# Turning the local attention result by whole-array matmuls instead of 64x64 tiles, under a newly written order of all steps

## The chip, the core and the metric

The kernel runs on one core of one Trainium2 chip. A core has a matrix engine (TensorE, here PE, with weight loads shown apart as PEld), a vector engine (VectorE, DVE), an engine for activation functions (ScalarE, ACT), a general engine (GpSimd, POOL), an engine that only issues and waits (SyncE, SP), and 16 DMA engines that move data. Each engine works through its own list of instructions in order, and waits on semaphores for the others. PE writes into PSUM, which here is used as eight banks of 512 float32 columns by 128 partitions; the other engines evacuate these banks into SBUF, the working memory.

The metric is the time of one execution on the device in microseconds (us), lower is better.

## What is computed

Eight batches of 576 positions. Attention with 8 heads of 64 runs in two forms that are added: over means of four neighbouring positions ("down"), and over a band of positions less than 4 apart ("local"). The result is the input `x` (576 by 512 for each batch) of a mixing block:

```
q_d, k_d, v_d = means over 4 positions                      # 144 rows
x      = repeat(softmax(q_d k_d^T / 8) v_d, 4) + softmax(band(q k^T / 8)) v
theta  = x @ w_theta
y      = w_tok_r @ (x * cos(theta)) + w_tok_i @ (x * sin(theta))
u      = x + y
out    = u + relu(u @ w_ch)
```

## The kernel before

**One list of words.** All work is written as steps, each a small function. The string `ORDER` (line 57) names some 1,190 steps in the order in which they are emitted. The first two letters are the kind of step; what follows is its place: the PSUM banks (`xt45`: banks 4 and 5), the engine (`v` DVE, `a` ACT, `g` POOL), or the staging slot for a load (one of 16 SBUF buffers, in base 36). Each kind counts through its batches and parts by itself, so the n-th `xt` is always the same piece of work, and only its position and place can differ. Every instruction is pinned behind the one before it on its engine. So `ORDER` sets each engine's list, each bank, each slot, and on which engine a copy, cast or mask is done. `wm` words are matmuls on zeros, which keep PE active at the start (`wm737`: bank 7, three of 512 columns and one of 7 x 64). `te` and `ts` switch ACT's function table.

**A batch, in kinds of steps.**

- Loads `lk`, `lq`, `lv`/`lw` (k, q, v) go to staging slots by SP's queue. `ck`, `cq`, `cv` cast them to bfloat16. `tp` turns k and q on PE, `ev` evacuates them to `kT`, `qT`. For batch 0, v goes by `l1`, `c1`, `t1`, `e1`, `x1`; for batch 7, q and k are turned by DMA (`dk`).
- Down form: `kd`, `qd` sum four columns (on DVE or POOL), `pv`, `vd` do that for v, `sd` gives scores, `ed` the exponentials, `nd` their product with v, `xn` divides, `xd`, `xc` turn the result into `xdT`.
- Local form: the 576 positions are cut into 10 windows of 64 rows that own 58 positions each (the last fewer); two windows make a chunk, so there are 5 chunks, and units of 2, 2 and 1 chunks. `ps` (L482) gives scores of a unit, `ex` the exponentials, `mk` masks them to the band (L503 and L505, on DVE or POOL), `po` (L515) multiplies by v, and `nm` (L523, L524) divides and writes `tmp`, which holds window rows of 4 heads on partitions 0 to 63 and of the other 4 on 64 to 127. `xt` (L537) turns `tmp` into two PSUM banks; `xa` (L545) adds the down result, each column four times, and writes `xT`, which has channels on partitions and positions on columns.
- Mixing: `th` (L556) multiplies by `w_theta`, `cs` (L561, L562) takes cosine and sine, `xm` or the DMA `dx` turns `x` back, `zz` forms the products. `tt`, `ct`, `zt`, `zp` or `dz` do the same for the last 64 positions. `mx` (L636) mixes tokens in 8 parts of 9 matmuls, `ua` (L641) adds `x`, `up`/`uc` or the DMA `du` turn `u`, `ch` (L666) projects, `rl` (L674) adds and clips, `st` stores. Two batches' last 64 rows go together: `ut`, `dt`, `ht` (L700), `rt` (L704), `ss`, `sr`. The last projection of all, batch 7's fourth, is done in two halves of 256 columns (`rl` and `rm`).
- Weights: `la`/`ca`, `lb`/`cb`, `lc`/`cc` load and cast; `wp`, `wc` turn the token weights.

Steps of several batches are interleaved, so that PE works on one batch's mixing while the other engines prepare the next batch's attention.

`ps`, `po`, `sd` and `xt` use PE in tiles of 64 rows by 64 columns, of which four fit in the array (`64*64` in the profile's rows); `pv` and `x1` use fewer columns (`128*32`, `128*64`). All other matmuls use the whole array or nearly.

Of the kernel before, what the change touches and what calls it, by code (L numbers as in the profile page):

```python
# [62 lines left out]
evv lw th0 th2 lv0 cbv lw zz cbg tt3 xm4 lv3 cs cbg cbv ct cbg cbg cs lvb lw lw wp0 wcv wp1 wcv ztg wp5 th3 wp1 lv8
wcv xm2 cbg xm0 zz zp7 tp45 cs qdg wp3 wp6 zz wcv lw zz wcv wcv zca eva wp7 wcv wp1 wca te wp0 wcv ps34 ps56 ex ex
ps12 mx0 lq1 cvg lk2 lka mx7 lqc mx3 qdv cvg ua lk7 ex ua lk0 mkv mkv kdg sd67 po45 nm sd12 lq4 cva lk5 lk9 cvg cvg ed
ed mx0 ua ua lq3 pv67 po45 po23 nm mx0 vda mkg nd67 lk8 nd45 lkb nm xn xn lq6 ckg ckg tp12 mx3 po45 ua lca ua nm cqg
cqg tp67 eva eva xd0 ckg ckg up1 lq7 po23 lvc xcv nm tp45 xt67 cqg mx0 cqg xt23 eva xt45 lv4 qdg kdg uca lw lv0 lw lw
lv3 lv1 lw lw xa xa tp67 cka ts ckg ckg th1 th2 xa th5 lk8 xm4 evv cs cqg xm1 ckv th3 zz tt4 up6 lq6 lqb cs zz tp12
xm7 ua cs ucv ct cs cqg eva te ztv xm6 zz zz mx0 ua tp34 zp7 tp56 ps12 zcv mx7 mx0 ex cvv kdg evv eva lk7 lk9 cvg lk4
qdg ua up7 uca sd12 mkv ps34 po56 ex ua ccv lcc lc5 kdg nm mkv mx0 sd34 ed po56 cvg cvg ua cqg mx7 nm ua ed mx0 ua lk2  # L70
cka cqg ps67 lqd lq0 cva po45 nm lca ex po23 ckg ckg nm pv01 lvb mx6 vda lk6 utv lw tp45 eva lv1 lw cca ccv nd01 nd23
ua xn xn qdg tp67 mx5 eva lv8 lv9 cqg cqg lw lw ccg ps34 qdg ps67 ua ps12 kdv ex ex xd0 lva xca lw mkg mkg lqc lq0 ch5
rl ckg ckg cvg cvg ch3 sd67 xt45 mkg ed rl ex ts mx0 xa xt67 po45 lv5 th1 cs xa nm ua tp23 th7 up4 up1 ucv xt56 xa mkv
lv4 ch0 eva po56 po23 cvg lq2 tt4 uca th1 cs th7 nm st nm xm2 lqb rl lq1 zz lqd ct cvg xm6 lw cqg ch5 cs zz cs cqa te
up0 up1 rl sd23 ucv po67 ch4 nm rl ch0 rl ucv tp67 lv7 ed cvg pv45 vdv lk8 lk9 eva st st tp23 eva xm0 ztg lk0 lka lw
xm1 zz zz zp7 ch6 zca lvc lv3 kdg nd45 xn nd23 ckg tp01 cva xn qdg utg mx7 cka ps23 rl kdg eva ps01 ua po45 mx6 up7 ex
ex lw lw lv8 nm qdg lw cqg po45 cqg ucv lvb lv2 lw sd23 sd01 lv5 ed mx7 lw lw ua tp23 nm xd4 ed ckg ckg xca st evv
tp01 eva mx6 mkg xt45 xt23 ua ua cva cvg cvg xt01 cka ts cvg xa xa mx7 th6 xa po45 nm pv23 tt0 th1 lk4 xm4 st st mkg
th5 vdv st cs nd23 ua zz ct cqg cqg ztg tp67 th4 cs dt po01 cs cs te xn evv po23 mx5 kdg qdg xm4 xm6 mx7 nm ps01 ex nm
ps23 ua lvd ua ex ch5 ps01 ex qdg zz lw lw xm7 zz rl kdg zp6 zz mkg nd23 xn lv1 lva lv3 mx5 zca sd67 lw ps01 ex po34  # L80
mx2 ua lw ed tp01 sd67 cva nm po34 eva cvv cvg ed lw up5 uca ua mx2 cvg nm cvg lvc xd3 ua pv04 xcv lk7 lk0 mx7 lq9 lq6
lq2 lqd lq8 lqb lq5 ckg ckg vda lq7 lw xt56 mkv cqg cqg po34 lk4 xt01 xa xa ch2 st cva ts lv6 th5 up6 ckg xm0 nm th1
tp34 cs ucv cs mkg rl eva mx6 ua ua th1 xt67 lk0 lk1 cs cqa po45 mkv xa nm ht3 rt tp67 th1 eva zz xm2 lv9 xm3 xm4 lw
lve zz zz ckg dk4 kdv mx0 cqg tp67 nd23 xn cs zz ua cqa eva mx1 nd67 xn cqa sr cqa cka tt2 ct dkb up4 cva cva ua mx0
mx7 ua cvg cvv uca te po01 nm qdg kdg qdg sd56 ed po23 ua ch4 rl xd0 ch1 ztg lw nm up7 ch4 uca xca po23 dz xt67 rl evg
ckg nm st st pv15 vda mx0 ps23 xa ex rl up1 up7 evg ua ucv mx6 uca ss ps01 ex xt45 cqa utg xa ua lv1 dk4 ps23 ex mx7
up0 uca th4 lvb sd56 mkv po23 lw lw xt01 utg dt ua dk7 cvv nm th7 du ed ts evg nd56 xa nd23 tt0 xn xn ct qdg mkv mkg
evv mx1 ztg xd2 up0 ua cs ch3 rl cs te mx4 ch7 qdg ps56 rl xcv ua mx1 ex cvg po23 po45 ua uca ps67 ex ht1 nm nm st st
rt cva ss mx0 ua po67 xt45 nm ps23 st xa ex ts du kdg th1 xm0 xm7 cs th6 cs xm4 zz zz zz ch5 rl kdg mx7 ua th0 po67 nm
cs te xt45 xa sd12 ch3 xm0 ch7 ch4 xt56 st ed sd12 mkg mkg ed ts zz dz lw mx0 lv1 du du cvv lw cvg th1 cs rl uta mx3  # L90
st rl rl xa dxb ua po45 po67 pv02 nm nm ua du mx1 vda ch4 dx mkg ua po23 po01 po67 rl sr nm mx5 ua mx4 tt5 dx1 du nm
nm nd23 xn nd01 st mx6 th7 mx2 cs xn xd3 mx0 ua ua xcv ua ua xt67 utv ct dx st st xt45 xt23 xa ch1 rl th0 ch6 ch1 ch7
# [8 lines left out]
def kernel(  # L101
# [161 lines left out]
    at = {}  # L263
# [261 lines left out]
                                in0=ps[:, :, :, 0:D], in1=r.unsqueeze(3).to_broadcast([P, 2, 4, D]), op=ALU.mult)  # L525

    def xt(b, u, w):
        ps = at["xt", b, u] = pair(w).rearrange("p k (x n) -> p (k x) n", x=2)
        for i, c in enumerate(UNITS[u]):
            t = tmp[(NCH * b + c) % NTMP]  # L530
            for g in range(2):
                n = 2 * c + g
                lo = STEP * n - W0[n]
                for j in range(4):
                    for hf in range(2):
                        r = slice(W * hf, W * hf + W)
                        nc.tensor.matmul(out=ps[W * (j % 2):W * (j % 2) + W, 2 * hf + j // 2,  # L537
                                                CH * i + STEP * g:CH * i + STEP * g + OWN[n]],
                                         lhsT=t[r, g, D * j:D * j + D], rhs=ident[r, W * hf + lo:W * hf + lo + OWN[n]],
                                         start=True, stop=True)  # L540

    def xa(b, u, w):
        lo = 2 * CH * u
        cnt = min(2 * CH, S - lo)
        nc.vector.tensor_tensor(  # L545
            out=xT[b % 2][:, :, lo:lo + cnt].rearrange("p e (m j) -> p e m j", j=4),
            in0=at.pop(("xt", b, u))[:, :, 0:cnt].rearrange("p e (m j) -> p e m j", j=4),
            in1=xdT[b % 2][:, :, lo // 4:(lo + cnt) // 4].unsqueeze(3).to_broadcast([P, 4, cnt // 4, 4]),
            op=ALU.add)


# [256 lines left out]
```

## Time and profile before

| | |
|---|---|
| time, median of 3 runs | 231.89 us (229.57, 231.89, 232.5) |
| span of the profiled execution | 232.2 us, 9404 instructions; no other time of that execution is given |
| PE busy | 217.7 us, 94%, 3943 matmuls seen |
| weight loads | 152.6 us, 66% |
| DVE busy | 187.7 us, 81% |
| ACT busy | 156.2 us, 67% |
| POOL busy | 145.0 us, 62% |
| HBM read, written | 33.98 MB, 9.44 MB |
| granted clock of PE | 0.993 of full on the mean |

The profile is one execution. Busy time of an engine is the time in which it had an instruction at work; matmuls overlap in the array, so their lengths are longer than the time from one start to the next, and a cost on PE is read from starts. The chain of work is the path that ended last, followed back from the end. A few matmul records are missing from the trace.

### The profile page before, as it was taken

What the parts mean: (1) busy time and instruction counts of PE and PEld (TensorE: products, weight loads), DVE (VectorE), ACT (ScalarE), POOL (GpSimd) and SP (SyncE); (2) the same over time, 40 slices, a digit from 0 to 9 for tenths busy, and PEclk for the clock granted to TensorE, in tenths of its full rate; (3) what the DMA queues carried; (4) which work ended last, traced back from release to release, by engine and by line L of the source; (5) the groups of instructions that cost most, each with busy time, mean ns of one, the idle gap of its engine ahead of it and who ended that gap; (6) DMA issues with size and microseconds to landing.
All of it is one profiled execution on the core that took longest, in us unless ns stands there. A gap on an engine that the chain in (4) does not pass through costs nothing.

```text
span 232.2 us, 9404 instructions
## 1 busy us (share of the span) xinstructions
PE 217.7 (94%) x3943; PEld 152.6 (66%) x3970; DVE 187.7 (81%) x367; ACT 156.2 (67%) x243; POOL 145.0 (62%) x192
## 2 busy tenths in 40 slices
PE   7997899999999999899999989989998999999992
PEld 3655678877877666776775675756655775668741
DVE  5699888999988799789968887698986978558473
ACT  4589799689988898898877978778788232430000
POOL 7689977879985999879963489598952001100000
PEclk9999799999999999999999999999999999999999
DMA  6999968997999689968999996892284358656587
GB/s 217 395 390 390 291 114 238 361 300 118 265 391 179 165 245 285 243 142 214 205 165 347 307 213 115 206 153 92 67 149 109 71 127 193 138 159 137 142 227 245
DMA packets 76795, 49.41 MB, mean 213 GB/s; under 512 B 61136, under 2 KB 61392, under 8 KB 76752
## 3 DMA queue, kind: packets, MB, share of 16 engines
q1 hardware_dynamic: 76096, 47.76, 81.9%
q10 hardware_dynamic: 656, 1.05, 1.3%
q8 instruction: 31, 0.51, 0.9%
q14 instruction: 12, 0.10, 0.1%
HBM read 33.98 MB, written 9.44 MB: 187 GB/s over the span
## 4 chain that ended last, share of the span: by engine, by line
PE 60%; DMA 10%; POOL 10%; issue 6%; ACT 5%; DVE 4%; SPq 4%; DVEq 0%; POOLq 0%; ACTq 0%
PE PS L636 21%; PE PS L666 9%; PE PS L556 8%; DMA st<-in_q_dram 6%; PE PS L302 4%; POOL two L329 3%; PE PS L515 2%; SPq L347 2%; DMA st<-in_k_dram 2%; PE PS L537 2%; DMA ur<-uT 2%; POOL q_tm L295 2%; PE PS L482 2%; PE PS L447 1%; PE PS L595 1%
## 5 line engine op out<-in xcount | busy, mean ns | idle before, releaser
L636 PE MATMUL PS<-WT,z 128*128 128x288 bf16 x576 | 78.0, 287 | 0.0
L636 PEld LDWEIGHTS <-z 128*128 128x128 bf16 x576 | 53.9, 98 | 15.9 <-issue 1.3
L641 DVE TENSOR_TENSOR uT<-PS,xT 128x288 bf16<-128x288 f32 x64 | 28.6, 452 | 12.7 <-PE PS L636 10.9
L561 ACT ACTIVATE cs<-PS,pihc 128x512 bf16<-128x512 f32 x32 | 22.0, 689 | 21.1 <-PE PS L556 13.4
L556 PE MATMUL PS<-wth,xT 128*128 128x512 bf16 x116 | 30.8, 383 | 0.7 <-issue 0.2
L666 PE MATMUL PS<-wch,uT 128*128 128x512 bf16 (+1 forms) x122 | 29.8, 373 | 0.9 <-issue 0.6
L524 DVE TENSOR_TENSOR tmp<-PS,rl 128x512 bf16<-128x512 f32 x40 | 27.7, 692 | 1.4
L545 DVE TENSOR_TENSOR xT<-PS,xdT 128x928 bf16<-128x928 f32 (+1 forms) x24 | 22.3, 952 | 3.7 <-PE PS L537 2.3
L674 DVE SCALAR_TENSOR_TENSOR osb<-PS,ur 128x512 f32<-128x512 f32 x28 | 19.1, 687 | 7.1 <-DMA ur<-uT 3.0
L490 ACT ACTIVATE pm<-PS 128x1024 bf16<-128x1024 f32 (+1 forms) x24 | 20.5, 880 | 6.2 <-PE PS L482 6.1
L577 POOL TENSOR_TENSOR zT<-xT,cst 128x512 bf16<-128x512 bf16 x7 | 9.7, 1383 | 20.6 <-ACT cst L574 20.6
L295 POOL CAST k_tm<-st 128x576 bf16<-128x576 f32 x23 | 15.1, 668 | 11.2 <-DMA st<-in_k_dram 11.1
L396 POOL CAST v_w<-st 128x512 bf16<-128x512 f32 x21 | 13.3, 651 | 10.6 <-DMA st<-in_v_dram 10.5
L770 ACT ACT_TABLE_LOAD x15 | 19.2, 1283 | 0.3
L666 PEld LDWEIGHTS <-uT 128*128 128x128 bf16 x132 | 11.9, 98 | 11.2
L562 ACT ACTIVATE cs<-PS 128x512 bf16<-128x512 f32 x32 | 19.1, 597 | 0.0
L556 PEld LDWEIGHTS <-xT 128*128 128x128 bf16 x128 | 11.7, 99 | 10.6 <-issue 0.6
L295 POOL CAST q_tm<-st 128x576 bf16<-128x576 f32 x23 | 15.4, 686 | 4.9 <-DMA st<-in_q_dram 4.7
L503 POOL TENSOR_TENSOR pm<-pm,band 128x512 bf16<-128x512 bf16 x16 | 18.3, 1164 | 0.0
L329 POOL TENSOR_TENSOR two<-qT 128x576 f32<-128x576 bf16 x14 | 16.5, 1177 | 0.7 <-ACT qT L315 0.4
L620 DVE TENSOR_TENSOR z<-PS,cs 128x1024 bf16<-128x1024 bf16 x24 | 15.8, 684 | 0.5 <-ACT cs L562 0.3
L437 ACT ACTIVATE pd<-PS 128x864 bf16<-128x864 f32 x16 | 13.8, 889 | 2.5 <-PE PS L426 2.5
(124 smaller groups left out, 422.9 us busy)
## 6 DMA issues: line engine op xcount, KB each, us to landing
st<-in_k_dram SPq DMA_DIRECT2D x32, 288.0 KB, 6.5
st<-in_q_dram SPq DMA_DIRECT2D x32, 288.0 KB, 6.3
st<-in_v_dram SPq DMA_DIRECT2D x70, 128.0 KB, 5.2
out_dram<-osb SPq DMA_DIRECT2D x26, 256.0 KB, 4.0
st<-in_v_dram SPq DMA_DIRECT2D x4, 288.0 KB, 3.5
st<-in_moe_w_tok_r_dram SPq DMA_DIRECT2D x4, 288.0 KB, 6.5
...
```

Of the source, the lines that this page charges most:

```text
L295: COPY[w](out=to, in_=of)
L329: nc.gpsimd.tensor_tensor(out=t, in0=src[:, :, 0:2], in1=src[:, :, 2:4], op=ALU.add)
L490: nc.scalar.activation(out=pm[(3 * b + u) % NPM][:, :, 0:n].rearrange("p e c j w -> p e (c j w)"), in_=at.pop(("ps", b, u))[:, :, 0:4 * W ...
L524: nc.vector.tensor_tensor(out=tmp[(NCH * b + c) % NTMP].rearrange("p g (j d) -> p g j d", d=D), in0=ps[:, :, :, 0:D], in1=r.unsqueeze(3).t ...
L545: nc.vector.tensor_tensor(out=xT[b % 2][:, :, lo:lo + cnt].rearrange("p e (m j) -> p e m j", j=4), in0=at.pop(("xt", b, u))[:, :, 0:cnt].r ...
L556: nc.tensor.matmul(out=ps, lhsT=xT[b % 2][:, dc, P * c:P * c + P], rhs=wth[:, dc, :], start=(dc == 0), stop=(dc == 3))
L561: nc.scalar.activation(out=t[:, 0, :], in_=ps, func=AF.Sin, bias=pihc, scale=1.0)
L562: nc.scalar.activation(out=t[:, 1, :], in_=ps, func=AF.Sin, bias=0.0, scale=1.0)
L636: nc.tensor.matmul(out=ps, lhsT=z[b % 2][:, j, P * dc:P * dc + P], rhs=WT[:, j, cols], start=(j == 0), stop=(j == 8))
L641: nc.vector.tensor_tensor(out=uT[b % 2][:, dc, cols], in0=at.pop(("mx", b, i)), in1=xT[b % 2][:, dc, cols], op=ALU.add)
L666: nc.tensor.matmul(out=ps[:, cols], lhsT=uT[b % 2][:, dc, P * c:P * c + P], rhs=wch[:, dc, cols], start=(dc == 0), stop=(dc == 3))
L770: nc.scalar.activation(out=idle, in_=pihc, func=TABLE[kind])
```

## The change

The step `xt` is written anew. Before, each window gives 8 matmuls of a 64x64 tile: the weights are 64 rows by 64 columns of `tmp`, the moving operand 58 columns of the identity. After, each window gives 2 matmuls on the whole array: the weights are all 128 rows by 128 columns of `tmp` (two heads of each half), and the moving operand is 58 columns of the identity's upper half and 58 of its lower half, 116 in all. Over the kernel `xt` has 640 matmuls and weight loads before, 160 after. The result stands in the two banks in another order of its four blocks, and `xa` reads it by another pattern. The two banks of an `xt` step need not be neighbours any more.

`ORDER` is replaced as a whole. The kinds and numbers of steps are the same but for `wm` (6 words before, 5 after). Positions, banks, slots and the engines of copies, casts, masks and means differ. No other function and no constant is changed.

```diff
 ORDER = """
-kcg l10 l11 l12 l13 kcv lk4 lq5 c1a wm7e0 kcg c1g t101 lk6 lk7 ckg c1a ckg c1v t123 e1a kcv e1v wm737 tp01 x12 cqa x13
-lq8 x14 cka x15 cqg evv cva lk9 tp67 ckg cvv cva lqa lqb tp01 lk1 cqg x14 cva wm521 evv evv cqa qdv tp23 cva la3 eva
-pv47 vda wm624 ps01 kdg la6 ps23 ex kdv ckg lq4 ex wm656 wm717 lq2 ps01 qdg lk5 sd67 mkv ckv cqg sd45 po23 ed lk8 cag
...
-mx4 ua ua ua sr mx7 mx6 mx5 ua ua ua ua du du ua ch7 ch6 ss ch5 rl rl ch7 ch6 ch4 ch3 du du st uta dt sta rl st rl ht7
-ch2 sta rl st rl sta rl st rt ssa sr rl sta rm su k0
+l10 l11 l12 lk3 l14 c1g lk5 lq6 kcg c1v lq7 wm090 t101 lk8 lk9 kcv c1v e1v lqa c1g cka ckg wm227 t123 cqg cqg e1a kcg
+ckg tp01 lq1 x14 ckg cqg cqg x15 tp23 x16 eva eva cvv kcv cvv lq0 lk3 lb4 lk5 lb6 lb7 x17 x14 tp01 cva cva wm523 tp67
+qdg eva eva cvv kdv qdg ckg pv45 wm215 ps01 vdv kdv la8 la9 lqa cba ckg cqg la1 lb2 lbb ex lk4 lac lqd ps67 cag cbg
+lb3 lk5 cbg lq0 cbg ex mkv wm247 sd01 sd45 ps67 po23 ed ed po01 lb8 ex lb7 lb2 lv6 mkv nm po45 tp23 nd67 nm cbg cqa
...
+mx7 mx6 ua mx7 ch1 ua ua ch0 du st ch7 du st ch6 rl ch1 ch2 du ss ch3 st du sr du st rl rl sta rl utg utg rl dt st sta
+rl ch1 st rl sta st ht0 rm k0 su rt sr rl ssa sta
 """
...
     def xt(b, u, w):
-        ps = at["xt", b, u] = pair(w).rearrange("p k (x n) -> p (k x) n", x=2)
+        ps = at["xt", b, u] = pair(w).rearrange("p k (x n) -> p k x n", x=2)
         for i, c in enumerate(UNITS[u]):
             t = tmp[(NCH * b + c) % NTMP]
             for g in range(2):
                 n = 2 * c + g
                 lo = STEP * n - W0[n]
-                for j in range(4):
-                    for hf in range(2):
-                        r = slice(W * hf, W * hf + W)
-                        nc.tensor.matmul(out=ps[W * (j % 2):W * (j % 2) + W, 2 * hf + j // 2,
-                                                CH * i + STEP * g:CH * i + STEP * g + OWN[n]],
-                                         lhsT=t[r, g, D * j:D * j + D], rhs=ident[r, W * hf + lo:W * hf + lo + OWN[n]],
-                                         start=True, stop=True)
+                for k in range(2):
+                    nc.tensor.matmul(out=ps[:, k, :, CH * i + STEP * g:CH * i + STEP * g + OWN[n]],
+                                     lhsT=t[:, g, P * k:P * k + P], rhs=identw[:, :, lo:lo + OWN[n]],
+                                     start=True, stop=True)
 
     def xa(b, u, w):
         lo = 2 * CH * u
         cnt = min(2 * CH, S - lo)
         nc.vector.tensor_tensor(
-            out=xT[b % 2][:, :, lo:lo + cnt].rearrange("p e (m j) -> p e m j", j=4),
-            in0=at.pop(("xt", b, u))[:, :, 0:cnt].rearrange("p e (m j) -> p e m j", j=4),
-            in1=xdT[b % 2][:, :, lo // 4:(lo + cnt) // 4].unsqueeze(3).to_broadcast([P, 4, cnt // 4, 4]),
+            out=xT[b % 2][:, :, lo:lo + cnt].rearrange("p (x k) (m j) -> p x k m j", k=2, j=4),
+            in0=at.pop(("xt", b, u))[:, :, :, 0:cnt].rearrange("p k x (m j) -> p x k m j", j=4),
+            in1=xdT[b % 2][:, :, lo // 4:(lo + cnt) // 4].rearrange("p (x k) m -> p x k m", k=2).unsqueeze(4)
+            .to_broadcast([P, 2, 2, cnt // 4, 4]),
             op=ALU.add)
```

More of the change, by code (lines that the diff above doesn't have):

```diff
@@ L63 @@
[L63 to L92, printed above, removed]
@@ new lines @@
+lw cs zz wcv ct ztg lw th3 wp2 lk3 lq5 lqd xm4 wp5 lk4 wp6 xm7 eva wcv zz wcv wp2 zp0 ps14 cs te qdg wcv zcv wcv zz
+ps35 wp6 wca qdg mx0 mx2 kdv cvg ex sd67 ps14 ckg ex ex ed cvg cva mkv ua mx3 po01 ua mkv nm sd45 po67 mx2 nm ua ed
+cvg cvg po45 po01 ua nm pv67 mx3 xt45 vda mkg ckg cqg ts nd67 nm ua nd01 xn mx3 xn lk0 lq1 lk2 lq7 lk8 tp67 cqg eva
+cka xd2 ua lv6 lq3 lq5 lw lv4 mx3 lkd xcv xt01 tp67 xa po45 th2 xa lkc lvb lv9 nm eva lw lqa ckg lw ckg cqg lw lq1 lc2
+qdg tp01 cs cqa xt45 th6 xm2 cqg evv xa th7 tt4 kdg xm5 cs ct ckv zz zz up6 ucv lv3 cqv tp01 ztv ua lw lc5 th2 xm6 cs
@@ new lines @@
+mx5 kdg zp7 ckg cvg lq6 lkd eva ckg lkc lc8 ps01 xm3 ua cs zcv zz tp45 ex zz up7 mx6 eva tp23 tp01 ua mkv eva uca evv
+mx6 qdg ps45 kdg cvg cqg po23 uta sd01 qdg ex cvv ed cva cqg mx7 ua nm ckg mx6 sd01 cqg ps23 po45 ex mkv ua ed nm ua
+mx7 up4 ua cva po23 uca ckg po01 mkg ccg pv56 vda up7 nm cca lvb lc4 lw lk9 mx4 lqa ucv nm tp23 nd01 nd67 mx5 xn ccg
+tp01 eva ua xn ps23 te qdg cqg cca ps67 ua evv ex xd5 ch4 lk7 lv1 rl xt23 lv6 lw lw lka lv8 lq2 lw lv4 xca xa ex cva
+xt01 mx5 kdg xa ua ch6 lw lqb lkc lv5 ps23 po01 sd47 ex ed th5 ch2 nm rl kdg cvg ckg mkg cvg ckg cs ts mkv rl up6 tp01
@@ new lines @@
+th7 xt23 evv uca cs th4 xm5 cs xa po23 po01 nm zz th6 up7 nm ucv tt2 tp45 cvv cs ch3 ch7 sd01 rl ckg cvg lq9 lv1 st
+lq7 lka lq4 lv6 st lw po36 rl ct eva pv45 ztg mkg ckg cqg cqa ed qdg xm7 nm ch2 zz vda xm3 up7 xm6 tp01 zz rl ucv ch3
+zp2 nd45 zz eva zcv cqa xn kdg nd01 tp67 mx2 eva cka xn ua ps01 po67 ps45 nm ex mx2 lw lv2 lqc lkb xd0 rl ex lw st qdg
+lw lva sd67 po13 sd45 mkg ua mx2 ed lw lv9 cvv nm cvg cqg ed ua xca uta mkg cvg ckg xt67 xa mx1 xt23 xt45 tp67 lq7 lk1
+lq5 lv8 lw th0 ts cqg ua xa up1 mx2 lv6 lq4 lw lvb lkd xa ua cqa eva uca cs xm6 st th7 lw tp01 dt lvc lq3 lq0 kdg cvg
@@ new lines @@
+zz cvv lw tp23 qdg ckg lk1 lw lk2 lva st evv ch6 cs eva pv45 lke lw rl po23 po01 st lvf vda nm th7 nm xm6 th4 nd23 tt5
+mx0 cs cs xn ct zz qdg ztg kdg ps45 po67 cqa ps23 mx1 ua nm xm0 zp6 xm7 ex nd45 ua zz xn ex zca mx1 ua zz ckg mkg po23
+ps45 sd06 cvg nm mx1 ua xd7 ex ed sd23 po45 mkg cqg ps06 ed mx1 ex nm cvg tp45 xt23 xca ua cva cqg ckg eva cvg xa cqg
+cvg ht1 xt67 mx0 po23 po45 xa rt pv67 mx1 ckg ua nm utg mkg vda ckg ts cva ua kdg tp23 mx6 evv nm lv9 lk6 lk1 lqb up7
+nd01 th2 xt45 ts cs xn ucv th3 xa tp01 xm2 tt7 ua cs ckv ct eva tp45 ch3 xm7 cka zz nd26 ztv eva mkg qdg zz xn cqg kdg
@@ new lines @@
+cqv rl qdg lw th0 th1 up4 xd5 xm2 mx6 mx3 st cva lw lk2 st ss cs lqc dk6 dz dkb lvf ckg ucv evg cva po04 xcv cs ua zz
+ua po67 sd12 nm ch5 xm0 nm up4 lw lq2 st mx3 lv9 sr lw rl zz ua ps67 ed te ex uca po12 ps05 nm ch3 mx1 rl xt67 up4 ua
+cva uca te xa xt23 mkg ch1 cqa ex up6 evg cvg uca xa rl mx7 ua ps45 sd01 po23 te ex pv67 cqv nm dk6 st st lvf vda ed
+th4 up5 lw lvc up2 th3 dk2 cs nd67 ch0 ch1 ucv xn qdg cva rl xt67 rl xa du uca cs lv9 evv nd45 eva mkg th0 lvb lw cs
+up6 xm7 mx2 tt3 utg qdg mkg uca xn zz ct mx4 ua ps01 ua po67 ps25 nm lw mx3 te ua ztv ex dt lw st lv2 lw dz ex du mx6
@@ new lines @@
+xd7 mx0 ua kdg po23 po45 cvg xcv mkg ps67 nm nm ua th1 ht2 xt45 rt mx0 xm2 xa kdg mkg ch3 ua ex cva zz rl sd45 po67
+cva nm cs utv ed mkg sd01 ch2 cva xm3 xm6 th7 te ed xt45 cs zz zz xa rl mx3 xt01 ua mx6 xa pv23 po01 po45 vda ts mx7
+nm ua dx2 dx mx2 dxb st st du dx du st nm po45 st du ua po01 po67 nm ua nm mx3 nm mx4 ch2 th5 nd67 ch0 ua xn ua zz rl
+cs th1 cs mx4 nd67 tt1 ch5 ct xt23 xn xd1 zz ua rl xcv ch6 rl xa mx7 zz th5 xt23 ch4 ztg ua cs xa th7 rl du xt23 dz du
+du th5 zz st xa sr dx2 mx6 tt2 mx3 th1 ch0 ss cs mx7 dx dxb st cs dx ts ct cs ua mx1 ch2 ua ch3 mx6 ua rl ua zz ua rl
@@ L97 @@
+zz th1 mx6 zz ua utg ztg cs du st du dz st du st dt mx0 zz ua rl mx6 mx7 mx2 mx0 ht1 ua ua mx7 rl ua rt ua ua mx1 ua
+mx7 mx6 ua mx7 ch1 ua ua ch0 du st ch7 du st ch6 rl ch1 ch2 du ss ch3 st du sr du st rl rl sta rl utg utg rl dt st sta
+rl ch1 st rl sta st ht0 rm k0 su rt sr rl ssa sta
 """
```

7 lines of the change are left out of this document (2 added, 5 removed).

## Prediction

> **What bounds the kernel now.** I read the page's first two parts, then the engines' busy time by stretches, because a share over the whole span mixes the filling of the pipeline with its steady part.
>
> ```profile
> PE 217.7 (94%) x3943; PEld 152.6 (66%) x3970; DVE 187.7 (81%) x367; ACT 156.2 (67%) x243; POOL 145.0 (62%) x192
> ```
> ```profile
> 0.00:37.00 37.00, 32.41 (x649) 22.42 (x654) 30.79 (x69) 28.33 (x43) 30.73 (x59) 0.95 0.90 292
> ...
> 80.00:100.00 20.00, 19.19 (x380) 13.71 (x381) 17.08 (x36) 17.25 (x25) 18.77 (x25) 1.00 0.94 243
> 100.00:120.00 20.00, 19.70 (x453) 14.21 (x453) 18.63 (x35) 16.56 (x26) 18.18 (x23) 1.00 1.07 191
> ```
> ```profile
> 25.00:37.00 12.00, 11.72 (x280) 9.38 (x282) 10.86 (x20) 11.03 (x18) 10.07 (x15) 0.86 0.78 191
> 37.00:220.00 183.00, 177.40 (x3257) 126.42 (x3279) 150.13 (x288) 127.48 (x200) 114.28 (x134) 1.00 0.84 196
> 220.00:232.20 12.20, 7.86 (x41) 3.79 (x39) 6.75 (x11) 0.40 (x1) 0.00 (x0) 1.00 0.74 227
> ```
>
> The columns are start:end, length, busy time of PE, weight loads, DVE, ACT and POOL, then granted clock, DMA share and GB/s. The chain of work shows the first `mx` steps:
>
> ```profile
> 36.96 3.42 PE PS L636 x27
> ```
>
> From there to 220 us PE is busy 177.4 of 183: only 5.6 us are free. So the middle of the kernel costs what PE's list of steps costs, and a new order can take at most 5.6 us of idle out of it. Before 37 us no engine is full: data arrives, and casts, transposes, evacuations and exponentials wait for one another. After 220 us what remains is the last projections and the way out.
>
> The changed steps are on PE, so I read PE's own timeline for how `xt` (L537) stands among its neighbours. The first column is the start, the second the modelled length; a step's cost is the difference of two starts.
>
> ```profile
> 79.01 0.67 PE L302 MATMUL PS<-ident,q_tm 128*128 128x128 bf16 x9
> 79.51 1.03 PE L556 MATMUL PS<-wth,xT 128*128 128x512 bf16 x4
> ...
> 80.91 0.31 PE L537 MATMUL PS<-ident,tmp 64*64 64x58 bf16 x16
> 81.16 1.04 PE L666 MATMUL PS<-wch,uT 128*128 128x512 bf16 x4
> ...
> 82.51 0.64 PE L568 MATMUL PS<-xT,wth 128*128 128x64 bf16 x16
> 82.99 1.89 PE L556 MATMUL PS<-wth,xT 128*128 128x512 bf16 x7
> ```
> ```profile
> 100.57 1.27 PE L636 MATMUL PS<-WT,z 128*128 128x288 bf16 x9
> 101.77 0.86 PE L537 MATMUL PS<-ident,tmp 64*64 64x58 bf16 x80
> 102.56 1.28 PE L636 MATMUL PS<-WT,z 128*128 128x288 bf16 x9
> ```
> ```profile
> 169.62 1.27 PE L636 MATMUL PS<-WT,z 128*128 128x288 bf16 x9
> 170.72 1.03 PE L556 MATMUL PS<-wth,xT 128*128 128x512 bf16 x4
> ```
>
> **The change on PE.** *Old matmuls.* 80 of them last 102.56 − 101.77 = 0.79 us and 16 last 81.16 − 80.91 = 0.25 us: 0.54/64 = 8.4 ns each, since four tiles work at a time, and 0.11 us for leaving the tiled form. *Entering it* costs the step ahead: nine `mx` matmuls take 1.10 us when a whole-array step follows (169.62 to 170.72) and 1.20 us when a tiled one does (100.57 to 101.77), 0.10 us more. So a run of neighbouring tiled steps pays 0.21 us once, whatever its length, and 640 matmuls cost 640 × 8.4 = 5.4 us beside that.
>
> *New matmuls.* 5 chunks × 2 windows × 2 halves × 8 batches = 160, with 128 by 128 weights and 116 columns streamed. No such form is in the trace. The nearest rows are whole-array matmuls that also load new weights each time: 128 columns, 9 in 79.51 − 79.01 = 0.50 us, 56 ns; 64 columns, 16 in 82.99 − 82.51 = 0.48 us, 30 ns. On the line between, 116 columns take 51 ns: 160 × 51 = 8.2 us, bounds 4.8 and 9.0. I take the line; the two pieces of 58 columns that each reads and writes I cost at nothing more, which the upper bound covers in part.
>
> *Runs of tiled steps.* I went through both lists and counted unbroken runs of `ps`, `po`, `sd`, `pv`, `x1` (and `xt` before) among the steps that issue matmuls: 51 before, 35 after. Part of this is `xt` itself, part is that the new list puts `po` beside `ps` and `sd` more often. 16 × 0.21 = 3.4 us go.
>
> PE's list thus changes by 8.2 − 5.4 − 3.4 = **−0.6 us**. All other PE steps are there in the same number. Of warming matmuls there were 30.1 units of 512 columns and are 20.8; they lie where PE would wait, so I cost them at nothing. If the cover fails, the price is the throttle: 25 to 37 us ran at 0.86 of the clock, 0.14 × 12 = 1.7 us lost. The new list may have no such stretch or a second one: ±1.7 us in the range.
>
> **The other engines.** Counted letter by letter, DVE loses three masks (`mk`), two means (`qd`), one evacuation (`ev`) and gains two `zt`; POOL gains three masks (one whole, two small) and the two means, and loses two `zt` and an `ev`.
>
> ```profile
> L503 POOL TENSOR_TENSOR pm<-pm,band 128x512 bf16<-128x512 bf16 x16 | 18.3, 1164 | 0.0
> L329 POOL TENSOR_TENSOR two<-qT 128x576 f32<-128x576 bf16 x14 | 16.5, 1177 | 0.7 <-ACT qT L315 0.4
> ...
> L295 POOL CAST k_tm<-st 128x576 bf16<-128x576 f32 x23 | 15.1, 668 | 11.2 <-DMA st<-in_k_dram 11.1
> ...
> L577 POOL TENSOR_TENSOR zT<-xT,cst 128x512 bf16<-128x512 bf16 x7 | 9.7, 1383 | 20.6 <-ACT cst L574 20.6
> ...
> L335 POOL TENSOR_TENSOR qd<-two 128x288 bf16<-128x288 f32 x14 | 9.3, 665 | 1.1
> ...
> L505 DVE TENSOR_TENSOR pm<-pm,band 128x1024 bf16<-128x1024 bf16 x8 | 7.0, 882 | 0.0
> ...
> L315 DVE COPY qT<-PS 128x1152 bf16<-128x1152 bf16 x5 | 6.7, 1348 | 0.8 <-PE PS L302 0.8
> ...
> L312 POOL COPY kT<-st 128x1152 bf16<-128x1152 bf16 x2 | 4.4, 2184 | 2.6 <-DMA st<-k_tm 2.6
> ...
> L321 DVE TENSOR_REDUCE qd<-qT 128x288 bf16<-128x1152 bf16 x2 | 2.7, 1348 | 0.0
> ...
> L674 DVE SCALAR_TENSOR_TENSOR st<-PS,ur 128x256 f32<-128x256 f32 x2 | 0.8, 420 | 0.2 <-PE PS L666 0.2
> ...
> L577 DVE TENSOR_TENSOR zT<-xT,cst 128x512 bf16<-128x512 bf16 x1 | 0.8, 753 | 0.2 <-ACT cst L574 0.2
> ...
> L704 DVE SCALAR_TENSOR_TENSOR st<-PS,utr 128x512 f32<-128x512 f32 x1 | 0.7, 692 | 0.2 <-PE PS L700 0.2
> ```
>
> DVE: 3 × 0.88 + 2 × 1.35 + 1.35 − 2 × 0.75 = 5.2 us less, casts and small copies moved both ways give about 1 back: 4 us less. POOL: a whole mask is two instructions, 2.33 us; 2.33 + 2 × 1.16 + 2 × (1.18 + 0.67) = 8.3 more, − 2 × 1.38 − 2.18 = 3.4 net, casts about +1. `xa` (L545) reads its banks by another pattern, the same 928 elements: nothing, since DVE has 33 us free beside PE; were each of the 24 instructions 0.1 us longer, DVE's gain would be smaller by 2.4.
>
> What DVE's relief is worth is read from PE's waits in the steady part (who waited, us in total, times, longest):
>
> ```profile
> PE PS L515 <- DVE pm L505: 0.8, 1, 0.8
> PE PS L302 <- POOL q_tm L295: 0.8, 1, 0.8
> PE PS L666 <- issue: 0.6, 4, 0.2
> PE PS L482 <- ACT kT L315: 0.6, 1, 0.6
> ...
> PE PS L515 <- DVE osb L674: 0.4, 1, 0.4
> PE PS L515 <- DVE xT L545: 0.3, 1, 0.3
> ```
>
> DVE holds PE for 0.8 + 0.4 + 0.3 = 1.5 us. I take half, **−0.7**; bounds 0 and −1.5.
>
> **Start.** Ahead of the first `mx` the old list gives POOL 20 casts, the new one 25, one mask less and one mean more, of which the last two follow the last cast that `mx` needs. That is 5 × 0.67 = 3.3 more, less a mask of 1.2 to 2.3: 1 to 2 us, against the 6.3 us (37 − 30.73) that POOL idled there. The loads up to the last token-weight block are the same blocks. PE's work up to there is the same within 0.3 us. I cost the start at 0; bounds −2 (the weight transposes now fill holes earlier) and +2 (POOL has no room for its DMA waits).
>
> **Queues.** All loads stay on SP's queue, stores on SP's and ACT's, equal in number. With the order, staging slots move too; a load waits for the cast that frees its slot, and the transposing DMAs (`du`, `dt`, `dx`, `dz`) hold whatever stands behind them. In both lists I followed each load from the last release ahead of it to its cast: the shortest distances, counted in PE's steps, are some 6 us in either, so I cost this at 0.
>
> **End.** Before, the last PE step is a projection in halves, then DVE does two halves. After, it is the tail projection `ht`, and behind it DVE does `rt` (0.69) and a half (0.42), 1.11 against 2 × 0.42 = 0.84, and both stores follow: **+0.4** with the later issue; bounds 0 and +0.8.
>
> **Sum.** Against the profiled span, 232.2: −0.6 − 0.7 + 0.4 = 231.3. The page gives no time beside its span; the span is 0.3 above the median of the runs shown (231.89), so **231.0 us** for a median. Own range 228 to 234: two or three of the terms at their bounds at once, not all.
>
> The Trainium skill, "TensorE: Matmul & The Clock Gate", section "Back-to-back issue gap", gives about 81 ns a matmul for a sustained stream of 128-column pairs of load and matmul. By it the new matmuls would be some 13 us (an estimate from that page) and the change a loss; the trace's 56 ns for just such pairs disagrees, and I go by the trace.
>
> **Rivals.**
> *The list is better than its sum* (227.0). PE's remaining idle of 5.6 us in the middle goes but for about 1, and half of the throttled stretch. 231.0 − (5.6 − 0.7 − 1) = 227.1. For: it is the only sizeable loss left, and DVE is freer. Against: those waits have four different engines behind them, and POOL, one of them, gets more. 0.22.
> *POOL becomes the bound* (236.9, slower). Each mask that goes from DVE to POOL lengthens the way from `ps` to `po` by 2.33 − 0.88 = 1.45 us, and casts for the next batch queue behind it. From 80 to 120 us POOL is busy 36.95 of 40. If the 8.3 us added come there and what it loses comes later, 8.3 − 3.05 = 5.2 us have no room, and DVE's relief isn't seen: 231.0 + 0.7 + 5.2. It decides from 3.05 us added to that stretch on. For: POOL's `zt` and `ev` of the last batch leave late. Against: the means are spread over batches. 0.14.
> *Weights pace the new matmuls* (238.5). If a load isn't hidden beside the matmul, each costs the load's own 98 ns:
>
> ```profile
> L568 PEld LDWEIGHTS <-wth 128*128 128x128 bf16 x128 | 4.6, 98 | 1.1 <-issue 0.3
> ```
>
> 160 × 98 = 15.7 instead of 8.2, +7.5. Against: this same row's matmuls follow at 30 ns. 0.04.
>
> **Chances.** Forecast 0.60, better list 0.22, POOL 0.14, weights 0.04. A difference under 2%, 4.6 us, is about what a measurement of this kernel can tell from none. Faster by more than that is under 227.3, slower over 236.5. Half of the second case and a little of the forecast lie below: faster 0.17; most of POOL's and the weights' lie above: slower 0.17; within 0.66. The range reaches down to 227.0, the better list's own time, and up to 236.2, short of POOL's full price.
>
> **What would show it.** `xt` as 8 matmuls in about 0.41 us with no longer step ahead of it; 35 tiled runs; PE in the steady part still over 96% busy; the first `mx` at 37 ± 2 us; DVE some 4 us less busy, POOL some 4 more. Wrong if PE's idle in the middle is under 2 or over 9 us, if the start moves by over 2 us, or if the new matmuls are not near 51 ns apart.

## The result, and the profile after

| | median us | runs | ratio to before, with 95% interval |
|---|---|---|---|
| before, beside it | 231.89 | 5, 229.49 to 232.5 | |
| changed kernel | 248.32 | 5, 245.14 to 250.29 | 1.0662 [1.0564, 1.076] |

The changed kernel is 6.6% slower; the prediction said no change. The ratio leaves out runs more than 1.5% above the fastest of their kernel (here the two longest of five), so it lies below the quotient of the medians. A time lies about 1.7 us above the span of the same execution (span 246.6, time 248.32). So the profile of before that the prediction rests on, span 232.2, was one of its longer executions: a second profile of it has a span of 230.1 and a time of 231.84.

The page's busy times and the stretches of the changed kernel:

```profile
PE 220.7 (89%) x3453; PEld 156.7 (64%) x3480; DVE 186.4 (76%) x362; ACT 157.7 (64%) x244; POOL 148.7 (60%) x199
```
```profile
37.00:220.00 183.00, 169.06 (x2810) 121.77 (x2818) 141.44 (x268) 130.14 (x207) 116.69 (x139) 0.98 0.79 180
```

No engine has much more to do than before (PE's 3.0 us more is mostly time at half clock, see below). PE's share fell from 94% to 89%, and in the stretch that the prediction used it is busy for 169.1 of 183 us: 13.9 us idle, where before had 5.6. From the first `mx` matmul to the last, by their starts (37.91 to 233.00 us, before 36.89 to 219.85), lie 195.1 us in place of 183.0, while 1.0 us is added ahead of it and 1.2 behind. Of the 12.1 us, 8.4 are idle time of PE (14.0 against 5.6), and most of the rest is a stretch at half clock. So the loss is stalls of PE in the middle. The largest piece, 124 to 132 us, on PE, ACT and DVE (start, length; in brackets the idle time before it and what ended that; three dots where rows are left out):

```profile
123.22 1.28 PE L634 MATMUL PS<-WT,z 128*128 128x288 bf16 x9
124.34 0.42 PE L466 MATMUL PS<-ident,xdn 72*128 72x72 bf16 x8
125.97 0.38 PE L426 MATMUL PS<-qd,kd 64*64 64x144 bf16 x12 [1.21 <-ACT pd L437]
...
126.99 0.22 PE L482 MATMUL PS<-qT,kT 64*64 64x64 bf16 x3 [0.42 <-issue]
127.14 2.34 PE L634 MATMUL PS<-WT,z 128*128 128x288 bf16 x9
131.22 1.14 PE L302 MATMUL PS<-ident,k_tm 128*128 128x128 bf16 x9 [1.74 <-DVE tmp L524]
```
```profile
125.03 0.89 ACT L437 ACTIVATE pd<-PS 128x864 bf16<-128x864 f32 x1 [0.70 <-DVE uT L639]
...
129.60 0.60 ACT L490 ACTIVATE pm<-PS 128x512 bf16<-128x512 f32 x1 [2.31 <-PE PS L634]
```
```profile
130.23 0.21 DVE L523 RECIPROCAL rl<-PS 128x8 f32<-128x8 f32 x1 [5.24 <-ACT pm L490]
```

Read with the banks of `ORDER` beside it, almost none of these waits has to do with the data. `ed` (L437) reads the scores of `sd06`, batch 5, in banks 0 and 6; it waits for `ua` (L639), which reads `mx` in bank 1. `sd23` (L426) writes banks 2 and 3 and waits for `ed`. `ex` (L490) reads `ps06` and waits for the end of `mx1` (L634). `nm` (L523) divides `po45`, banks 4 and 5, and waits 5.2 us for that `ex`; and `tp45` on PE (L302) waits for `nm`. But for this last, each of these waits joins a read of banks 0 and 6 to a step in a bank **between** the two.

The new order gives 13 steps two banks that are not neighbours (`xt03`, `ps14` twice, `ps35`, `sd47`, `po36`, `po13`, `sd06`, `ps06`, `nd26`, `po04`, `ps05`, `ps25`); the old one gives such a pair to none. The evacuation reads both banks in one instruction. What places the waits in the built program takes such a read as one access to everything from the first bank to the last: there, the first `ex` of batch 1, reading banks 1 and 4, waits for the last matmul of an `mx` in bank 2. I call these waits **false**.

The stall has a second price: from 127.1 to 133.9 us the granted clock was one half, and the nine `mx` matmuls at 127.14 last 2.34 us in place of 1.28. The Trainium skill, "TensorE: Matmul & The Clock Gate", section "What's actually happening", describes windows of about 3.4 us after which the rate is halved or restored. The lengths agree (6.8 us is two such windows). The same page of the Trainium skill, section "HAM oscillation — how this bites in real kernels", puts the limit at gaps of over about 3.4 us; here pieces of 1.21 and 0.42 us in the 3.4 us ahead of 127.1 went with the drop.

### The profile page after: what moved, and what is told of

Read it like the earlier page. It is cut to its first block, busy times and chain, and to the rows that moved or that the text cites. A ratio compares the mean times of both kernels' runs of the same rounds, so it can differ in the third digit from the quotient of the medians.

```text
span 246.6 us, 8415 instructions
## 1 busy us (share of the span) xinstructions
PE 220.7 (89%) x3453; PEld 156.7 (64%) x3480; DVE 186.4 (76%) x362; ACT 157.7 (64%) x244; POOL 148.7 (60%) x199
## 4 chain that ended last, share of the span: by engine, by line
PE 55%; DMA 12%; DVE 9%; ACT 7%; issue 6%; SPq 5%; POOL 4%; DVEq 0%; ACTq 0%; POOLq 0%
PE PS L634 22%; PE PS L554 7%; PE PS L664 7%; PE PS L302 3%; DMA st<-in_moe_w_tok_r_dram 3%; PE PS L535 3%; DMA st<-in_q_dram 3%; DMA st<-in_k_dram 2%; DMA st<-in_v_dram 2%; PE PS L515 2%; DVE tmp L524 2%; SPq L603 2%; PE PS L593 2%; PE PS L698 1%; DVE pm L505 1%
## 5 line engine op out<-in xcount | busy, mean ns | idle before, releaser
L634 PE MATMUL PS<-WT,z 128*128 128x288 bf16 x576 | 79.6, 289 | 2.9 <-ACT pm L490 1.6
L634 PEld LDWEIGHTS <-z 128*128 128x128 bf16 x576 | 54.6, 98 | 18.6 <-issue 3.7
L639 DVE TENSOR_TENSOR uT<-PS,xT 128x288 bf16<-128x288 f32 x64 | 28.8, 451 | 13.7 <-PE PS L634 12.3
L554 PE MATMUL PS<-wth,xT 128*128 128x512 bf16 x115 | 31.4, 379 | 2.9 <-ACT pd L437 1.2
L490 ACT ACTIVATE pm<-PS 128x1024 bf16<-128x1024 f32 (+1 forms) x24 | 20.7, 882 | 10.4 <-PE PS L482 5.6
L329 POOL TENSOR_TENSOR two<-qT 128x576 f32<-128x576 bf16 x16 | 18.4, 1148 | 14.7 <-ACT qT L312 6.9
L542 DVE TENSOR_TENSOR xT<-PS,xdT 128x928 bf16<-128x928 f32 (+1 forms) x24 | 22.6, 952 | 4.8 <-PE PS L535 2.3
L503 POOL TENSOR_TENSOR pm<-pm,band 128x512 bf16<-128x512 bf16 x18 | 20.9, 1185 | 4.7 <-ACT pm L490 4.7
L575 POOL TENSOR_TENSOR zT<-xT,cst 128x512 bf16<-128x512 bf16 x5 | 5.8, 1155 | 26.5 <-ACT cst L572 26.5
L295 POOL CAST k_tm<-st 128x576 bf16<-128x576 f32 x26 | 18.7, 726 | 4.5 <-PE PS L634 2.9
L329 POOL TENSOR_TENSOR two<-kT 128x580 f32<-128x580 bf16 x13 | 15.2, 1171 | 3.6 <-ACT kT L315 3.3
L654 POOL COPY ut<-uT 128x256 bf16<-128x256 bf16 x5 | 2.0, 404 | 24.3 <-DVE uT L639 24.3
L523 DVE RECIPROCAL rl<-PS 128x8 f32<-128x8 f32 x40 | 8.0, 201 | 10.6 <-ACT pm L490 5.2
L437 ACT ACTIVATE pd<-PS 128x864 bf16<-128x864 f32 x16 | 14.1, 891 | 1.9 <-PE PS L426 1.2
```

What stands on the lines that cost most here:

```text
L329: nc.gpsimd.tensor_tensor(out=t, in0=src[:, :, 0:2], in1=src[:, :, 2:4], op=ALU.add)
L490: nc.scalar.activation(out=pm[(3 * b + u) % NPM][:, :, 0:n].rearrange("p e c j w -> p e (c j w)"), in_=at.pop(("ps", b, u))[:, :, 0:4 * W ...
L503: EW[w].tensor_tensor(out=t[:, x], in0=t[:, x], in1=m[:, x], op=ALU.mult)
L542: nc.vector.tensor_tensor(out=xT[b % 2][:, :, lo:lo + cnt].rearrange("p (x k) (m j) -> p x k m j", k=2, j=4), in0=at.pop(("xt", b, u))[:, ...
L554: nc.tensor.matmul(out=ps, lhsT=xT[b % 2][:, dc, P * c:P * c + P], rhs=wth[:, dc, :], start=(dc == 0), stop=(dc == 3))
L634: nc.tensor.matmul(out=ps, lhsT=z[b % 2][:, j, P * dc:P * dc + P], rhs=WT[:, j, cols], start=(j == 0), stop=(j == 8))
```

## Experiments

The theory, F: the loss is false waits around far pairs. The rivals: L, the order itself; X, the new matmuls; P, POOL's masks. Each ratio is to runs of before made beside that kernel, with a 95% interval.

**1. All far reads split.** The changed kernel; for each of the 13 steps the reading instruction becomes two, one per bank. In the same way for `ed`, `xn`, `nm`, `xa`:

```diff
+    def parts(key):
+        return [slice(0, 1), slice(1, 2)] if key in FAR else [slice(0, 2)]
...
-        nc.scalar.activation(out=pm[(3 * b + u) % NPM][:, :, 0:n].rearrange("p e c j w -> p e (c j w)"),
-                             in_=at.pop(("ps", b, u))[:, :, 0:4 * W * n], func=AF.Exp, scale=SCL)
+        ps = at.pop(("ps", b, u))
+        for e in parts(("ps", b, u)):
+            nc.scalar.activation(out=pm[(3 * b + u) % NPM][:, e, 0:n].rearrange("p e c j w -> p e (c j w)"),
+                                 in_=ps[:, e, 0:4 * W * n], func=AF.Exp, scale=SCL)
```

> The changed kernel, with only the readers of the 13 steps whose two PSUM banks are not neighbours (`ps14`, `ps35`, `po36` and so on) done as two instructions, one for each bank. Theory F (an access that spans two distant banks is ordered against everything in the banks between, so those readers wait for strangers and strangers for them): those waits go; PE's idle from the first mixing step on falls from some 20 us to under 9, the span from 246.6 to 231 to 237 although 13 to 26 short instructions are added. Rival L (the list itself is badly matched to the chip, POOL above all): the span stays at 244 or more. Rival X (the new matmul form or its evacuation is what costs): stays at 244 or more.

Measured: 236.68 us, ratio 1.0274 [1.0215, 1.0334]; the profiled execution has a span of 234.0. The stretch again, and the place of the long stall (the same steps, 119 to 124 us in this kernel):

```profile
37.00:220.00 183.00, 179.99 (x2877) 129.57 (x2875) 149.06 (x290) 130.54 (x215) 117.00 (x139) 1.00 0.87 191
```
```profile
119.70 0.42 PE L482 MATMUL PS<-ident,xdn 72*128 72x72 bf16 x8
120.06 0.38 PE L437 MATMUL PS<-qd,kd 64*64 64x144 bf16 x12
120.27 0.30 PE L535 MATMUL PS<-v_w,pm 64*64 64x65 bf16 x16
120.40 0.50 PE L499 MATMUL PS<-qT,kT 64*64 64x64 bf16 x16
120.83 1.28 PE L661 MATMUL PS<-WT,z 128*128 128x288 bf16 x9
121.95 0.67 PE L312 MATMUL PS<-ident,k_tm 128*128 128x128 bf16 x9
```

(Lines lie higher because of the added code.) The steps now follow one another with no gap, the clock stays whole, and PE is busy 180.0 of 183 us. F holds for the larger part; a rest of 2.7% stays.

**2. The old order with the new `xt`**, and **3. the new order with the old `xt`.** In 2 only the string `ORDER` is the old one; in 3 `xt` has its 8 tiled matmuls a window again, each half of the heads in a bank of its own, and `xa` reads the banks by a pattern that fits; the order is the new one.

> The old list of steps with the new matmul form and the new evacuation pattern. All its bank pairs are neighbours. Theory F and rival L: PE's list costs 160 x 52 ns - 640 x 8.4 ns = 2.9 us more and two runs of tiled steps fewer (0.4 us less), so 2 to 3 us over the kernel before: a ratio of 1.00 to 1.02. Rival X: a ratio of 1.04 or more.

> The new list with the old 64x64 matmuls. Theory F and rival L: as slow as the changed kernel or slower, since 56 runs of tiled steps stand in place of 35 (21 x 0.21 = 4.4 us more) against 2.9 us of streaming less: a ratio of 1.06 to 1.08 to the kernel before. Rival X: a ratio of 1.00 to 1.02.

Measured: 231.76 us, 1.0083 [1.0054, 1.0113] for 2; 248.15 us, 1.0696 [1.0615, 1.0778] for 3. The new matmuls alone cost 0.8%, 1.9 us; the new order alone costs as much as the whole change (7.0% against 6.6%, the intervals overlap). X falls: it carries at most the 0.8%.

**4 to 6. Which pairs.** Only some of the 13 split: the six of batches 5 to 7 (`sd06`, `ps06`, `nd26`, `po04`, `ps05`, `ps25`); the three of batch 3 (`sd47`, `po36`, `po13`); the four at the start (`xt03` and `ps` of batch 1). Against the kernel of run 1, for batch 3:

```diff
-        if b - a > 1:
+        if b - a > 1 and key in (('sd', 3, 0), ('po', 3, 2), ('po', 3, 4)):
             FAR.add(key)
```

> As the first, but only six of the 13 readers are split, those of batches 5 to 7 (`sd06`, `ps06`, `nd26`, `po04`, `ps05`, `ps25`). Theory F: the stall of 124 to 132 us (DVE idle for 5.2 us behind one exponential) goes with its half-clock stretch, the early ones at 38 to 45 us stay: 4 to 9 us less than the changed kernel, a ratio of 1.025 to 1.05. Rivals L and X: a ratio of 1.055 or more.

> The changed kernel with one read per bank for only three steps: sd of batch 3, first part (banks 4, 7), and po of batch 3, third and fifth chunk (3, 6 and 1, 3). F: the stall at 124 to 132 us goes, and the half clock behind it at 127 to 134 us. Between the first mx of batch 3 and that of batch 4 lie 33.3 us in the changed kernel and 26.2 with all 13 split: 7 us less, ratio 1.03 to 1.05. If the groups of far pairs only hide one another (the next one in the list gives the time back): ratio 1.055 to 1.07.

> The changed kernel with one read per bank for only four steps: xt of batch 0, second unit (0, 3), and ps of batch 1, all units (1, 4; 3, 5; 1, 4). F: the stall at 40 to 42 us goes. From the first mx of batch 0 to that of batch 1 are 25.0 us in the changed kernel and 22.3 with all 13 split: 2.7 us less, some 0.6 behind it; ratio 1.045 to 1.06. If nothing is had by these alone: 1.066.

Measured: late pairs 243.74 us, 1.0571 [1.0483, 1.0658]; batch 3 244.07 us, 1.0613 [1.0536, 1.069]; batch 1 245.24 us, 1.0665 [1.0595, 1.0736]. All three gain less than I expected from F; the first even lies where I had put L and X, the others where I had put no gain. The times of these kernels scatter by 2 to 3 us from run to run, and the intervals overlap that of the changed kernel, so the ratios decide nothing here; only the traces tell the groups apart. A table of the time from the first `mx` matmul of one batch to the first of the next, from PE's timeline, one execution each (for batch 3 its longest, 249.94 us, where the other three took 242.9 to 245.0):

| us from batch to batch | 0-1 | 1-2 | 2-3 | 3-4 | 4-5 | 5-6 | 6-7 | 7-last mx |
|---|---|---|---|---|---|---|---|---|
| before, second profile | 23.1 | 33.0 | 23.3 | 28.0 | 30.2 | 23.7 | 11.4 | 8.7 |
| changed | 25.0 | 36.4 | 23.9 | 33.3 | 29.9 | 23.5 | 13.6 | 9.6 |
| all split | 22.3 | 35.8 | 23.4 | 26.2 | 28.4 | 23.4 | 13.8 | 9.6 |
| late split | 26.4 | 36.4 | 23.9 | 30.2 | 28.4 | 23.6 | 13.6 | 9.6 |
| batch 3 split | 26.4 | 35.5 | 23.2 | 34.8 | 29.9 | 23.5 | 13.6 | 9.6 |
| batch 1 split | 22.6 | 35.4 | 23.9 | 30.8 | 29.9 | 23.7 | 13.7 | 9.6 |
| old order, new `xt` | 23.7 | 33.3 | 23.6 | 27.2 | 29.9 | 23.1 | 11.4 | 8.7 |
| the same, banks renamed (7) | 23.9 | 33.5 | 23.5 | 35.2 | 33.7 | 25.4 | 11.4 | 8.7 |
| the same, renamed and split (8) | 23.1 | 33.5 | 23.5 | 27.2 | 30.7 | 23.2 | 11.4 | 8.7 |

Two of the groups give time back in a column of their own: batch 1's pairs in 0-1, the late pairs in 4-5 and, once the gap and the half clock described next are taken off, in 3-4 (30.2 − 2.6 − 1.7 = 25.9). My expectation for batch 3 was put in the wrong column: its attention is prepared between the `mx` of batches 1 and 2, where 0.9 us went (though 1.0 went there with batch 1's pairs alone, so this gain is not its own); the stall at 124 to 132 us belongs to batch 5. What spoils the sum is the half clock. In the profiled executions of the late and of the batch 3 kernel, which both keep batch 1's pairs, it came at 43.4 us, and in both again at 128.7 us, 3.4 or 6.8 us each time. In the late kernel it followed a gap that is no wait for data, in the midst of one `ps` step:

```profile
126.11 0.48 PE L499 MATMUL PS<-qT,kT 64*64 64x64 bf16 x13
129.15 0.26 PE L499 MATMUL PS<-qT,kT 64*64 64x64 bf16 x3 [2.56 <-issue]
```

The last three matmuls of the step come 2.6 us late, and the profile names nothing that they waited for. The same gap, at the same step, is 0.4 us in the changed kernel, absent with all split, and 2.2 us in run 10 below. The traces point to PE's own instructions, which come by a queue of their own, in this kernel in 27 packets of 16 KB:

```profile
q8 instruction: 27, 0.44, 0.8%
```

27 packets for 6,974 recorded instructions of PE (before: 31 for 7,929) are some 256 to a packet, an estimate from these counts. The 14 profiles show 14 such gaps of 0.3 us or more after 20 us. Each ends 1.2 to 1.7 us after a packet has landed (here one landed at 127.58), and 12 of them stand at the same place, 193rd to 195th, when PE's recorded list is counted off by 256; the other two are in profiles with records missing. That PE stood waiting for its next instructions is therefore likely; no run varied it.

**7. The reverse: far pairs in the old order.** The kernel of 2, and from the second unit of batch 4's `xt` on the names of banks 1 and 2 are exchanged, so that 01 becomes 02 and 23 becomes 13. No step moves and no datum depends on another one. **8.** adds the split reads to that. One line of `ORDER` in 2 and in 7:

```diff
-lve zz zz ckg dk4 kdv mx0 cqg tp67 nd23 xn cs zz ua cqa eva mx1 nd67 xn cqa sr cqa cka tt2 ct dkb up4 cva cva ua mx0
+lve zz zz ckg dk4 kdv mx0 cqg tp67 nd13 xn cs zz ua cqa eva mx2 nd67 xn cqa sr cqa cka tt1 ct dkb up4 cva cva ua mx0
```

> The order of before with the new xt, in which the names of banks 1 and 2 are exchanged from the second unit of batch 4's xt on (at a place where neither holds anything). Every step stands where it stood and every true dependency is as it was; but 18 pairs that were neighbours (01, 23) are now 0 and 2, or 1 and 3. F (a read of two distant banks counts as one access to all banks between, and so waits and makes wait falsely): slower than the same order with its own names (1.0083 of before) by 2 to 12 us, ratio 1.015 to 1.06, with waits of DVE's and ACT's reads of [0, 2] and [1, 3] on matmuls and reads in the bank between. L and X (the order of the steps, or the new matmuls, are the loss): the same as without the renaming, 1.003 to 1.013.

> The order of before with new xt and banks 1 and 2 exchanged (1.065), and now each of its 18 far pairs read by one instruction per bank. F: the false waits go, and with them all but the price of 18 added reads: 1.008 to 1.018, as the same order with its own banks (1.0083). If the loss there came from the banks themselves or from the place of the exchange: 1.05 or more.

Measured: renamed 244.69 us, 1.065 [1.0591, 1.071], a little above what F gave; renamed and split 232.41 us, 1.0109 [1.0049, 1.0169]. The stretches from the first `mx` matmul to the last, renamed and then split too:

```profile
36.75:232.06 195.31, 183.61 (x2866) 131.53 (x2858) 150.93 (x288) 128.02 (x200) 114.79 (x135) 0.99 0.74 182
```
```profile
35.73:217.05 181.32, 180.61 (x2865) 129.70 (x2858) 152.69 (x313) 128.11 (x204) 116.42 (x135) 1.00 0.80 196
```

PE's 11.7 us of idle (195.31 − 183.61) become 0.7. One of the false waits in the renamed kernel, on DVE, ACT and PE:

```profile
137.40 0.69 DVE L458 TENSOR_TENSOR xdn<-PS,rd 72x512 bf16<-72x512 f32 x1
```
```profile
138.19 0.69 ACT L559 ACTIVATE cs<-PS,pihc 128x512 bf16<-128x512 f32 x1 [3.56 <-DVE xdn L458]
```
```profile
139.41 1.26 PE L634 MATMUL PS<-WT,z 128*128 128x288 bf16 x9 [2.28 <-ACT cs L560]
```

`cs` takes the cosine of `th2`, bank 2; it waits 3.6 us until `xn` has read `nd13`, banks 1 and 3, and `mx` waits for `cs` through `zz`. This settles F: the same steps in the same order lose 5.6% by the names of two banks, and get all but 0.3% of it back when each bank is read by itself. That 0.3% lies inside the intervals, and with it the price of the split: 18 steps, but 29 more instructions, since `xn` and `nm` read their banks twice (DVE x313 in place of x288, ACT x204 in place of x200). What the new order costs beside its far pairs, rival L, is the 1.9% between runs 1 and 2.

**9 to 11. What is left.** All split is 1.0274, the old order with the same `xt` 1.0083. Their profiles differ by 4.4 us: the first `mx` 0.8 later (37.03 against 36.27), from there to the last `mx` matmul 2.0 more (182.96 against 180.92), the way out 1.6 longer (14.01 against 12.41). Three tries at it. 9: the last projection in a bank that is free.

```diff
-rl ch1 st rl sta st ht0 rm k0 su rt sr rl ssa sta
+rl ch4 st rl sta st ht0 rm k0 su rt sr rl ssa sta
```

> All 13 split as in the first experiment, and the last projection goes to bank 4 in place of bank 1, where PE waited 0.86 us (1.03 us from start to start above the normal) for DVE's read of an earlier projection. Theory E (part of what is left over, 1.027, is this wait at the end): 0.4 us less if DVE's own list of reads then sets the end, 0.9 us if PE does; ratio 1.022 to 1.027. Theory N (the end hangs on the last transposing DMA or the stores): no difference, 1.027.

Measured: 237.01 us, 1.0314 [1.0229, 1.0398]. PE's last matmul comes 7.7 us after the last `mx` in place of 8.7, and the end 14.1 in place of 14.0: nothing gained, as theory N had it. DVE waits at that place:

```profile
DVE st L699 <- DMA out_dram<-osb: 1.9, 1, 1.9
```

The releaser named is a store; by the built program this clip of batch 7 waits for the four turns `du`, and the fourth stood behind stores in SP's queue. 10 puts the turns ahead of three stores:

```diff
-mx7 mx6 ua mx7 ch1 ua ua ch0 du st ch7 du st ch6 rl ch1 ch2 du ss ch3 st du sr du st rl rl sta rl utg utg rl dt st sta
+mx7 mx6 ua mx7 ch1 ua ua ch0 du st ch7 du st ch6 rl ch1 ch2 du du ch3 du ss st sr st rl rl sta rl utg utg rl dt st sta
```

> The previous kernel (all 13 reads split, last projection in bank 4; 1.0314), and in SP's queue at the end the last two turns of u (du of batch 7, third and fourth part) and the words behind them stand ahead of three stores (ss, one st, sr) in place of between them. Theory S (what is left at the end is SP's queue: the fourth turn is issued 2.8 us after the last mx, and DVE's first clip of batch 7 waits 1.9 us for it): the fourth turn is issued some 2 us earlier, from the last mx to the end of the span 12.3 to 13.0 us in place of 14.1, ratio 0.005 to 0.008 lower. Theory N (the end hangs on the amount of the stores): 14.1 us as before.

Measured: 239.79 us, 1.0394 [1.0302, 1.0485]; from the last `mx` to the end 15.0 us, the wrong way. The wait has moved to the clip before:

```profile
DVE osb L699 <- DMA out_dram<-osb: 2.5, 1, 2.5
```

It writes one of five output buffers, whose store I had just sent to the back. (The rest of this run's loss is the gap in the midst of `ps`, with a half clock at 123.2 us.) 11: the five masks that the new order moves to POOL go back to DVE in the all-split kernel.

> All 13 reads split (1.0274), and the five masks that the new order gives to POOL and the old one to DVE go back to DVE (batch 3 third unit, batch 5 first and third, batch 6 first and second). Theory P (POOL is what is left in the middle; PE waits 0.66 us for its mask at 84 us): 0.5 to 2 us less, 1.019 to 1.025, and no wait of PE for POOL in the middle. Theory M (many small waits for many engines; DVE gets 3.5 us more and PE's waits for DVE grow): within 0.5 us, 1.025 to 1.03.

Measured: 237.3 us, 1.0327 [1.0246, 1.0408]. No gain, so P falls; the waits for POOL in the middle are gone, and DVE's grew (from start to start, `sd` at 151 us is 0.5 us late by DVE and `up` at 92 us 0.7 in place of 0.3). Gaps in the midst of a step take 1.4 us of this execution and 0.2 of the all-split one; without them the middle is 183.1 us against 182.7, still no gain.

**The kernel before, again.**

> The kernel before, unchanged, for a second profile of it: the one that the prediction rests on had a span of 232.2 us and 3.4 us at half clock at 24.9. If that one was a slow execution, this one has a span near 228 and PE is idle for less than 5.6 us between the first and the last mx; if not, 232 again.

```profile
36.34:217.70 181.36, 178.61 (x3287) 126.17 (x3279) 150.38 (x288) 127.63 (x200) 114.94 (x135) 1.00 0.84 198
```

Span 230.1, between the two that I had named, no half clock before the end, and 2.8 us of idle in the middle.

## Why the prediction was wrong

Term by term:

- **PE's list** was right in its prices, but its sum does not show. The new matmuls, forecast 51 ns, from the changed kernel's timeline:

```profile
79.49 1.00 PE L535 MATMUL PS<-ident,tmp 128*128 128x116 bf16 x16
80.33 1.26 PE L634 MATMUL PS<-WT,z 128*128 128x288 bf16 x9
```

  16 in 80.33 − 79.49 = 0.84 us, 52.5 ns. Entering a tiled run costs 0.09 us at the median and leaving it some 0.12 (forecast 0.10 and 0.11), and the counts of runs are as forecast, 51 and 35. At these prices the 14 runs fewer of all split against run 2 (35 against 49) are worth 14 × 0.21 = 2.9 us; PE's busy time in the middle is only 0.5 less (180.4 and 180.0 us), and against the second profile of before (178.6) it is 1.3 more, where the forecast was 0.6 less. What took up the saving is not known. The old order with the new `xt` loses 1.9 us, against 8.2 − 5.4 less two runs, 2.4. The weights did not pace the new matmuls.
- **DVE and POOL:** DVE 186.4 us busy against 187.7 (forecast 4 less, 1.3 came), POOL 148.7 against 145.0 (forecast some 4 more, 3.7 came). Neither decides, and nothing of the relief shows in the time.
- **The start** held: first `mx` at 37.91 us, forecast 37 ± 2. **The end** was forecast 0.4 longer, 0.8 at most; it is 1.2 longer (233.0 to 246.6, 13.6 us, against 12.4).
- **The step that failed is the idle time in the middle.** I had it bounded by the 5.6 us that were there and took "a new order can take at most 5.6 us of idle out of it" as if it could add little. It went to 14.0 us, past the 9 that I had named as a sign of being wrong, and PE was busy for 92% of the steady part, not for over 96%. Under queues I followed loads to casts, and under waits the data, and came to 0. The banks that the new order names I never went through, though the change says that a pair need not be neighbours. This term is +8.9 us by the ratios (1.0662 − 1.0274 of 230, give or take 2.6), 12.6 by the two profiled spans, of which 3.4 is the half clock of that execution.
- **The base** was off as well: I set the span of 232.2 beside the median of 231.89, but times lie 1.7 us above spans, so that median goes with a span of some 230.2. Half of the 5.6 us of idle belonged to that one execution; the second profile has 2.8.
- The rest, 1.9% between all split and run 2, was not forecast either. It is shared out over start, middle and way out; the four largest waits of PE left in the middle are 0.35 to 0.56 us each, for ACT, DVE and POOL. Three tries at parts of it gained nothing, so its cause is not settled.
- **Rivals.** The better list did not show: idle grew. POOL as the bound: in the middle of the all-split kernel it holds PE up by 0.5 us, and run 11 got nothing for its relief. What ended on the slow side was a mechanism that I had not listed.
